# Transposes by the DMA crossbar, joined half chunks and loads cast by DMA in a retention and MLP kernel

## The chip, the cores and the metric

The kernel runs on one core of a Trainium2 chip. A core has five engines with their own instruction streams: TensorE (PE, with weight loads shown apart as PEld), VectorE (DVE), ScalarE (ACT), GpSimd (POOL) and SyncE (SP). Each takes its instructions in order and waits at semaphores. DMAs are issued from SP's and POOL's streams in this kernel and run on sixteen DMA engines that all queues share. The metric is the device time of one execution in microseconds. The time before is 395.73 us, the median of three runs (395.54 to 396.46).

## The reference

There are 8 batches, 8 heads, 576 positions and a head size of 64. First comes retention: scores of q and k, masked to the lower triangle and weighted by a decay per head, times v. The heads side by side give x with 512 columns. Then a mixer of rank 32 over the positions adds to x, which gives u, and an MLP of width 2048 with a ReLU adds to u.

```python
scores = scale * np.matmul(q, k.transpose(0, 1, 3, 2))
gamma = 1.0 - 2.0 ** (-5.0 - np.arange(H, dtype=np.float32))
rel = pos[:, None] - pos[None, :]
Dmat = np.where(rel >= 0, gamma[:, None, None] ** rel[None, :, :], 0.0)
x = np.matmul(scores * Dmat, v)          # heads side by side: (8, 576, 512)
xt = x.transpose(0, 2, 1)
h = xt @ U @ V                           # over the positions, rank 32
u = x + h.transpose(0, 2, 1)
out = u + np.maximum(u @ w_ch1, 0.0) @ w_ch2
```

All inputs and the output are float32; the matrix products run in bfloat16.

## The kernel before

**Decay and state.** The decay is split into a factor of the row and one of the column. v is multiplied on load by `vscale` (the column's factor and the scale), and the result of a chunk by `qscale` (the row's factor). What is left inside a chunk is a triangle of ones, and what comes from earlier chunks is q times a running state, the sum of k transposed times v over those chunks. So a batch is walked in chunks of 128 positions. 576 is four and a half times 128: an even batch ends with a half chunk in partitions 0 to 63, an odd batch begins with one in partitions 64 to 127 (`is_half`, `rows_of`), and two batches of a pair lie in the output as nine full row blocks.

**The front of a batch**, in `attention_items` and `mixer_items`, is a list of small steps for PE, each with its followers on other engines:

- `T(c)`, line 202: eight PE transposes turn a chunk's q and k, head pair by head pair, into one PSUM tile `pst`; ACT copies it to SBUF as `qkT` (line 216).
- `ST(c)`, line 219: four matmuls add k transposed times v to the state in PSUM (`pss`); DVE copies it through a mask `bdm` that keeps the blocks of one head each, as `s_sb` (line 232).
- `SC(c)`, line 238: eight matmuls with 64 contraction rows give the scores, `psc`; DVE multiplies by the triangle, as `ret` (line 257).
- `RV(c)`, line 264: eight matmuls ret x v and four matmuls q x state (128 rows, since the masked state has zeros) gather in `po`; DVE scales to `xt` (line 287).
- `MA(c)`, `MH(c)`, `MT(c)`, lines 319 to 356: the mixer's product with U into `psa`, one copy `a_sb` by ACT, the product with V into `ph`, an addition on DVE that gives `ut`, then four PE transposes into `pu` and an ACT copy into `uT` (line 354).

**The MLP of a batch**, in `mlp_items`: `Y1` takes four matmuls per block of 128 hidden columns from `uT`, with an ACT ReLU; `Y2` takes sixteen matmuls per 128 rows, then DVE adds `ut` and SP stores the 256 KB result. An even batch has four row blocks, an odd one five.

**The order of the work.** PE's order is the program's order (`manual_schedule`): `interleave` mixes the MLP of batch b with the front of batch b + 1 in proportion to estimated costs. The orders on the other engines and on SP are chosen by the framework's scheduler when the program is built. `T` runs two steps ahead of `RV` of the same chunk. Tiles come from pools with fixed numbers of buffers; where a buffer is still in use, the writer waits.

**Loads.** `load_chunk`, line 171: SP loads k, q and v of a chunk as float32 into a staging tile (four buffers), in pieces of 256 bytes; DVE casts q and k to bfloat16 (line 184), POOL scales v (line 185). The weights are loaded by POOL's queue, which casts them while copying (lines 149 and 156). Batches 0 and 1 and the weights are loaded first; the loads of batch b + 2 are placed ahead of the MLP of batch b, and the scheduler runs them as buffers come free (nine of `qkv`).

Of the kernel before, what the change touches and what calls it, by code (L numbers as in the profile page):

```python
# [12 lines left out]
ALU = mybir.AluOpType  # L13
PE = mybir.EngineType.PE


def interleave(main, fill):
# [5 lines left out]
    while i < len(main) or j < len(fill):  # L23
        if j >= len(fill) or (i < len(main) and dm / tm <= df / tf):
            dm += main[i][0]
            main[i][1]()
            i += 1
        else:
            df += fill[j][0]
            fill[j][1]()  # L30
            j += 1
# [3 lines left out]
def kernel(  # L35
# [22 lines left out]
    NC = 5  # L58
    assert S == 4 * P + HALF and B % 2 == 0

# [7 lines left out]
    qkT_pool = ctx.enter_context(tc.tile_pool(name="qkT_pool", bufs=3))  # L68
# [4 lines left out]
    half_pool = ctx.enter_context(tc.tile_pool(name="half_pool", bufs=2))  # L73
# [5 lines left out]
    ps_t = ctx.enter_context(tc.tile_pool(name="ps_t", bufs=1, space=bass.MemoryType.PSUM))  # L79
    ps_sc = ctx.enter_context(tc.tile_pool(name="ps_sc", bufs=1, space=bass.MemoryType.PSUM))  # L80
    ps_s = ctx.enter_context(tc.tile_pool(name="ps_s", bufs=1, space=bass.MemoryType.PSUM))
    ps_o = ctx.enter_context(tc.tile_pool(name="ps_o", bufs=1, space=bass.MemoryType.PSUM))
# [5 lines left out]
    bdm = consts.tile([P, P], BF16, name="bdm")  # L88
    pos = consts.tile([P, NC, H], FP32, name="pos")
    lngt = consts.tile([P, NC, H], FP32, name="lngt")  # L90
    qscale = consts.tile([P, NC, H], FP32, name="qscale")
    vscale = consts.tile([P, NC, H], FP32, name="vscale")
    lnb = consts.tile([P, 1], FP32, name="lnb")
    U_A = consts.tile([P, NC, P], BF16, name="U_A")
    U_B = consts.tile([P, NC, P], BF16, name="U_B")
    Vbig = consts.tile([P, HALF + S + HALF], BF16, name="Vbig")
# [3 lines left out]
    qkvh = [consts.tile([P, 3, H, D], BF16, name=f"qkvh{p}") for p in range(2)]  # L100
    qkTh = [consts.tile([P, 2 * NHP, P], BF16, name=f"qkTh{p}") for p in range(2)]
    reth = [consts.tile([P, H, P], BF16, name=f"reth{p}") for p in range(2)]

    def early_consts():
        make_identity(nc, ident)
        make_upper_triangular(nc, tri, val=1.0, diag=True)
        nc.gpsimd.memset(lnb, math.log(scale))
        nc.gpsimd.iota(
            pos, pattern=[[P, NC], [0, H]], base=0, channel_multiplier=1,
# [4 lines left out]
        nc.vector.tensor_tensor(out=lngt, in0=lngt, in1=pos, op=ALU.mult)  # L114
        nc.scalar.activation(out=qscale, in_=lngt, func=AF.Exp, bias=0.0, scale=1.0)
        nc.scalar.activation(out=vscale, in_=lngt, func=AF.Exp, bias=lnb, scale=-1.0)
        nc.vector.memset(bdm, 0.0)
        for s in range(2):
            nc.vector.memset(bdm[s * HALF:(s + 1) * HALF, s * HALF:(s + 1) * HALF], 1.0)

    def zero_halves():
        for p in range(2):
            nc.vector.memset(qkTh[p], 0.0)
            nc.vector.memset(reth[p], 0.0)
            z = slice(HALF, P) if p == 0 else slice(0, HALF)
            nc.vector.memset(qkvh[p][z, :, :, :], 0.0)

    def late_consts():
        nc.vector.memset(U_A, 0.0)
        nc.vector.memset(U_B, 0.0)  # L130
        nc.vector.memset(Vbig, 0.0)
# [4 lines left out]
        nc.gpsimd.dma_start(out=U_A[0:HALF, 4, 0:R], in_=moe_U[4 * P:S, :])  # L136
        nc.gpsimd.dma_start(out=U_B[HALF:P, 0, 0:R], in_=moe_U[0:HALF, :])
# [54 lines left out]
    def attention_items(b, qkv, x_tiles, pair):  # L192
# [4 lines left out]
        def half_cols(c):  # L197
            if not is_half(b, c):
                return slice(0, P)
# [288 lines left out]
```

## Time and profile before

| What | Value |
|---|---|
| median of three runs | 395.73 us (395.54 to 396.46) |
| the profiled execution | 396.42 us, of which the span of its instructions is 394.6 us |
| busy: PE, weight loads, DVE, ACT, POOL | 348.4, 200.0, 183.1, 156.2, 64.2 us |
| first MLP matmul | 52.84 us |
| first ReLU of the MLPs of batches 0 to 7 | 54.7, 95.4, 142.4, 182.7, 229.6, 269.9, 316.9, 356.3 us |
| PE transposes of q and k | 320 matmuls, evicted by 40 ACT copies of 1.02 us |
| PE transposes of u | 144 matmuls, evicted by 36 ACT copies of 0.60 us |
| DMA queue of SP | 117696 packets, 37.8 MB |
| DMA queue of POOL | 5744 packets, 4.3 MB written |
| read from HBM, written to it | 36.92 MB, 9.44 MB |

The busy table gives each engine's busy time; a busy PE is not PE at its peak, since matmuls are pipelined and their ends are modelled. The forty slices show where in the span an engine is busy. The groups of instructions give one line of the program, its operands and shapes, how often it runs, its busy time with the mean duration of one in nanoseconds, and the idle time ahead of it with what ended that. The DMA issues give the median time from issue to landing. The chain of waits is followed back from the last instruction.

### The profile page before, as it was taken

To read this page: it belongs to the slowest core of one execution; us is meant where nothing else is said; L and a number is where in the kernel's file an instruction comes from. 1 tells how busy PE (TensorE), PEld (TensorE's weight loads), DVE (VectorE), ACT (ScalarE), POOL (GpSimd) and SP (SyncE) were. 2 spreads that over 40 slices of the span, in tenths; PEclk is the share of its full clock that TensorE was granted. 3 is DMA by queue.
4 is the path that set the end of the run, shared out by engine and by line. 5 is a ranking of instruction groups with operands and counts; after the bars stand their busy time and mean duration, and the time that the engine had idled before them with its cause. 6 is when DMAs were issued, how large, how long until landed. Compare 5 with 4: busy or idle time off the path is not lost. (4 is left out here: it accounts for less than half of the span.)

```text
span 394.6 us, 6659 instructions
## 1 busy us (share of the span) xinstructions
PE 348.4 (88%) x2784; PEld 200.0 (51%) x2784; DVE 183.1 (46%) x249; ACT 156.2 (40%) x279; POOL 64.2 (16%) x83
## 2 busy tenths in 40 slices
PE   1244489999999999899999999899999999999996
PEld 0233245446774455446764455346764455456642
DVE  4436326655456555753557445743334533540021
ACT  2121147305770156216760266117750276027700
POOL 6486123301321212210122002200000000000000
PEclk9999959999999999999999999999999999999999
DMA  8999999726995599485149500011001100010012
GB/s 157 217 184 197 198 224 212 131 69 166 223 209 124 150 207 213 98 196 139 25 97 207 140 28 1 28 42 40 2 2 55 55 27 2 28 53 27 2 53 81
DMA packets 123471, 42.49 MB, mean 108 GB/s; under 512 B 114705, under 2 KB 118833, under 8 KB 123441
## 3 DMA queue, kind: packets, MB, share of 16 engines
q1 hardware_dynamic: 117696, 37.76, 43.4%
q0 software_dynamic: 5744, 4.31, 7.2%
q8 instruction: 22, 0.36, 0.4%
q14 instruction: 9, 0.07, 0.1%
HBM read 36.92 MB, written 9.44 MB: 117 GB/s over the span
## 5 line engine op out<-in xcount | busy, mean ns | idle before, releaser
L390 PEld LDWEIGHTS <-w_sb 128*128 128x128 bf16 x768 | 70.4, 98 | 39.1 <-issue 4.7
L185 POOL TENSOR_TENSOR qkv<-stage_t,vscale 128x512 bf16<-128x512 f32 x32 | 34.7, 1085 | 128.3 <-DMA stage_t<-in_v_dram 65.3
L257 DVE TENSOR_TENSOR ret<-psc,tri 128x1024 bf16<-128x1024 f32 x32 | 39.1, 1221 | 9.3 <-PE psc L246 9.1
L328 ACT ACTIVATE a_sb<-psa 128x512 bf16<-128x512 f32 x8 | 4.8, 597 | 97.2 <-PE psa L322 97.2
L184 DVE CAST qkv<-stage_t 128x1024 bf16<-128x1024 f32 x32 | 30.9, 966 | 24.2 <-PE po L270 12.1
L232 DVE TENSOR_TENSOR s_sb<-pss,bdm 128x512 bf16<-128x512 f32 x32 | 22.1, 689 | 41.5 <-PE pss L225 41.5
L216 ACT ACTIVATE qkT<-pst 128x1024 bf16<-128x1024 bf16 x32 | 32.8, 1024 | 20.1 <-PE pst L207 19.1
L287 DVE TENSOR_TENSOR xt<-po,qscale 128x512 bf16<-128x512 f32 x32 | 22.0, 688 | 33.3 <-PE po L277 25.0
L207 PE MATMUL pst<-ident,qkv 128*128 128x128 bf16 x256 | 21.3, 231 | 15.4 <-DVE qkv L184 14.7
L207 PEld LDWEIGHTS <-qkv 128*128 128x128 bf16 x256 | 18.1, 104 | 22.1 <-DVE qkv L184 15.5
L344 DVE TENSOR_TENSOR ut<-ph,xt 128x512 bf16<-128x512 f32 x32 | 22.0, 690 | 11.9 <-PE ph L335 11.7
L270 PE MATMUL po<-qkv,ret 128*128 128x64 bf16 x256 | 13.7, 200 | 8.2 <-DVE ret L257 8.2
L270 PEld LDWEIGHTS <-ret 128*128 128x128 bf16 x256 | 11.6, 102 | 16.9 <-DVE ret L257 13.8
L225 PE MATMUL pss<-qkv 128*128 128x128 bf16 x112 | 11.6, 231 | 6.7 <-POOL qkv L185 6.7
L351 PE MATMUL pu<-ident,ut 128*128 128x128 bf16 x128 | 13.0, 227 | 4.3 <-DVE ut L344 3.8
L351 PEld LDWEIGHTS <-ut 128*128 128x128 bf16 x128 | 10.0, 101 | 12.7 <-DVE ut L344 5.2
L335 PE MATMUL ph<-a_sb,Vbig 128*128 128x512 bf16 x40 | 14.8, 392 | 0.7 <-ACT a_sb L328 0.7
L225 PEld LDWEIGHTS <-qkv 128*128 128x128 bf16 x112 | 9.2, 103 | 11.1 <-issue 6.8
L246 PE MATMUL psc<-qkT 64*128 64x128 bf16 x256 | 13.6, 229 | 0.0
L246 PEld LDWEIGHTS <-qkT 64*128 64x128 bf16 x256 | 7.7, 98 | 11.2 <-issue 11.2
L401 PEld LDWEIGHTS <-y_4127 128*128 128x128 bf16 x80 | 7.8, 98 | 9.3
L277 PE MATMUL po<-s_sb,qkT 128*128 128x128 bf16 x112 | 11.5, 229 | 0.0
(541 smaller groups left out, 615.7 us busy)
## 6 DMA issues: line engine op xcount, KB each, us to landing
out_dram<-o_sb SPq DMA_DIRECT2D x36, 256.0 KB, 2.1
stage_t<-in_k_dram SPq DMA_DIRECT2D x32, 256.0 KB, 4.8
stage_t<-in_q_dram SPq DMA_DIRECT2D x32, 256.0 KB, 4.9
stage_t<-in_v_dram SPq DMA_DIRECT2D x32, 256.0 KB, 5.0
w_sb<-in_moe_w_ch_dram POOLq DMA_DIRECT2D x16, 128.0 KB, 6.7
w_sb<-in_moe_w_ch_dram POOLq DMA_DIRECT2D x8, 256.0 KB, 10.0
stage_t<-in_k_dram SPq DMA_DIRECT2D x8, 128.0 KB, 3.8
stage_t<-in_q_dram SPq DMA_DIRECT2D x8, 128.0 KB, 3.8
```

What stands on the lines that cost most here:

```text
L184: nc.vector.tensor_copy(out=t[rows, 0:2, :, :], in_=f[rows, 0:2, :, :])
L185: nc.gpsimd.tensor_tensor(out=t[rows, 2, :, :], in0=f[rows, 2, :, :], in1=vscale[rows, c, :, None].to_broadcast([L, H, D]), op=ALU.mult,)
L207: nc.tensor.transpose(pst[:, j * NHP + hp, :], t[:, j, 2 * hp:2 * hp + 2, :].rearrange("p h d -> p (h d)"), ident,)
L216: nc.scalar.activation(out=qkT, in_=pst, func=AF.Copy)
L232: nc.vector.tensor_tensor(out=s_sb, in0=pss, in1=bdm[:, None, :].to_broadcast([P, NHP, P]), op=ALU.mult,)
L246: nc.tensor.matmul(psc[:, hl, hp, 0:n], qkT[pb:pb + HALF, NHP + hp, :], qkT[pb:pb + HALF, hp, cols], start=True, stop=True,)
L257: nc.vector.tensor_tensor(out=rv[:, :, :, cols], in0=psc[:, :, :, 0:n], in1=tri[:, None, None, cols].to_broadcast([P, 2, NHP, n]), op=ALU. ...
L270: nc.tensor.matmul(po[:, h * D:(h + 1) * D], ret[:, h, :], t[:, 2, h, :], start=(h == 0), stop=True, skip_group_check=True,)
L287: nc.vector.tensor_tensor(out=xt[rows, :].rearrange("p (h d) -> p h d", d=D), in0=po[rows, :].rearrange("p (h d) -> p h d", d=D), in1=qsca ...
L344: nc.vector.tensor_tensor(out=ut[rows, :], in0=ph[rows, :], in1=x_tiles[c][rows, :], op=ALU.add)
L351: nc.tensor.transpose(pu[:, cc, :], u_tiles[c][:, cc * P:(cc + 1) * P], ident)
L390: nc.tensor.matmul(ps[:, 0:n], w1_sb[:, cc, f * P:(f + 1) * P], uT[:, cc, t0:t0 + n], start=(cc == 0), stop=(cc == NCC - 1),)
```

## The change

Five things are changed together.

1. Nine chunks of 128 rows are walked per pair of batches. The fifth (`XC` = 4) holds the last 64 rows of the even batch and the first 64 of the odd one. Its scores are masked by `trix`, which also cuts across the two halves. The state starts anew at this chunk, from `vx`, a copy of v with the first half zeroed, and q x state uses `qTx`, a copy of q transposed with the second half zeroed; both copies are made by POOL. Group A of a pair is chunks 0 to 4, group B chunks 5 to 8, and the MLPs stay at four and five row blocks.
2. From the second group on, q and k, and u, are transposed by DMAs that SP issues, SBUF to SBUF, in place of PE and ACT. The first group keeps PE transposes, in `ps_big`.
3. q x state is computed next to the scores, in `SC`, as eight matmuls with 64 contraction rows that read only a head's own block of the state. So the mask `bdm` goes, and ACT copies the state in place of DVE. The two heads of a pair go to different PSUM banks of `po`.
4. From the third group on, the loads are issued by POOL and cast while they are copied, straight into `qkv`; POOL then scales v in place. The first two groups are still staged.
5. POOL's order is now the program's order too. The weights come in another order (the first four w1 blocks after the fourth chunk, the others after the first front). `RV` lags one step instead of two, in the first front none; the front mixed into the first MLP begins after 35% of it.

```diff
-def interleave(main, fill):
+def interleave(main, fill, lead=0.0, end=1.0):
...
-        if j >= len(fill) or (i < len(main) and dm / tm <= df / tf):
+        if j >= len(fill) or (
+            i < len(main) and dm / tm <= lead + (end - lead) * df / tf
+        ):
...
-    qkT_pool = ctx.enter_context(tc.tile_pool(name="qkT_pool", bufs=3))
+    qkT_pool = ctx.enter_context(tc.tile_pool(name="qkT_pool", bufs=6))
...
+    def scale_v(t, f, p, c):
+        nc.gpsimd.tensor_tensor(
+            out=t[:, 2, :, :], in0=f[:, 2, :, :],
+            in1=vscale[:, c, :, None].to_broadcast([P, H, D]), op=ALU.mult,
+        )
+        if c == XC:
+            nc.gpsimd.tensor_copy(out=vx[p % 2][HALF:P, :, :], in_=t[HALF:P, 2, :, :])
+
+    def load_chunk(p, c, cast_dma):
+        t = qkv_pool.tile([P, 3, H, D], BF16, tag="qkv", name="qkv")
+        if cast_dma:
+            for j, dram in ((1, k), (0, q), (2, v)):
+                for rows, b, t0 in parts(p, c):
+                    L = rows.stop - rows.start
+                    nc.gpsimd.dma_start(
+                        out=t[rows, j, :, :],
+                        in_=dram[b, :, t0:t0 + L, :].rearrange("h s d -> s h d"),
+                    )
+            scale_v(t, t, p, c)
+            return t
...
         def T(c):
             t = qkv[c]
-            pst = ps_t.tile([P, 2 * NHP, P], BF16, tag="ps_t", name="pst")
-            for j in range(2):
+            qkT = qkT_pool.tile([P, 2 * NHP, P], BF16, tag="qkT", name="qkT")
+            st["qkT", c] = qkT
+            if not pe_transpose:
+                nc.sync.dma_start_transpose(
+                    out=qkT, in_=t[:, 0:2, :, :].rearrange("p j h d -> p (j h d)")
+                )
+                return
...
         def ST(c):
...
-            nc.vector.tensor_tensor(
-                out=s_sb, in0=pss, in1=bdm[:, None, :].to_broadcast([P, NHP, P]),
-                op=ALU.mult,
-            )
+            nc.scalar.activation(out=s_sb, in_=pss, func=AF.Copy)
...
         def SC(c):
...
+            po = ps_o.tile([P, 2, 512], FP32, tag="ps_o", name="po")
+            st["po", c] = po
+            if c > 0:
+                s_sb = st["s", c - 1]
+                qT = qkT
+                if c == XC:
+                    qT = qTx[p % 2]
+                    nc.gpsimd.tensor_copy(
+                        out=qT[:, :, 0:HALF], in_=qkT[:, 0:NHP, 0:HALF]
+                    )
+                for hp in range(NHP):
+                    for hl in range(2):
+                        pb = hl * HALF
+                        nc.tensor.matmul(
+                            po[:, hl, hp * D:(hp + 1) * D],
+                            qT[pb:pb + HALF, hp, :],
+                            s_sb[pb:pb + HALF, hp, pb:pb + HALF],
+                            start=(hp == 0), stop=True, skip_group_check=True,
+                        )
...
         def MT(c):
-            pu = ps_t.tile([P, NCC, P], BF16, tag="ps_t", name="pu")
+            dst = st["uT", par][:, :, (c - c0) * P:(c - c0 + 1) * P]
+            if not pe_transpose:
+                nc.sync.dma_start_transpose(out=dst, in_=st["u", c])
+                return
...
+    with tc.manual_schedule(engines={PE, POOL}):
+        early_consts()
+        for c in A_CH:
+            sts[0]["qkv"][c] = load_chunk(0, c, False)
+            if c == 1:
+                load_mixer()
+            if c == 3:
+                load_w1([0])
+        interleave([], front_items(0, 0, True, 0))
+        load_w1(range(1, dff // W1B))
+        load_w2()
+        load_group(0, 1, False)
+        groups = [(p, par) for p in range(NP) for par in range(2)]
+        for g, (p, par) in enumerate(groups):
+            if g + 2 < len(groups):
+                load_group(*groups[g + 2])
+            fill = front_items(*groups[g + 1]) if g + 1 < len(groups) else []
+            interleave(mlp_items(p, par, sts[p]), fill, 0.35 if g == 0 else 0.0)
```

## The prediction

> **What bounds the kernel now.** I read the busy table and the 40 slices first. TensorE (PE) is 88% busy; only the first slices leave it idle, and there the DMA row is full.
>
> ```profile
> PE 348.4 (88%) x2784; PEld 200.0 (51%) x2784; DVE 183.1 (46%) x249; ACT 156.2 (40%) x279; POOL 64.2 (16%) x83
> ...
> PE   1244489999999999899999999899999999999996
> ...
> DMA  8999999726995599485149500011001100010012
> ```
>
> Next the timeline about the first MLP matmul: the MLP begins at 52.84 us, and its matmuls of 512 columns start 0.43 us apart, twice as far as later; the clock records stand at a half until 57.7 us.
>
> ```profile
> 52.84 1.87 PE L390 MATMUL ps_y_553<-uT_474,w_sb 128*128 128x512 bf16 x4 [0.69 <-ACT uT_474 L354]
> ```
>
> Stages (columns: window, length, busy time of PE, weight loads, DVE, ACT, POOL, granted clock, DMA share, GB/s): the half clock in the second, and one stage later on where PE stands 1.9 us.
>
> ```profile
> 40.00:50.00 10.00, 5.36 (x29) 2.52 (x30) 3.35 (x6) 1.54 (x3) 2.08 (x2) 0.87 1.08 203
> 50.00:60.00 10.00, 8.80 (x50) 4.85 (x48) 3.35 (x6) 5.14 (x8) 2.58 (x3) 0.62 1.09 221
> ...
> 160.00:170.00 10.00, 8.11 (x79) 3.99 (x78) 8.02 (x8) 1.02 (x2) 2.90 (x3) 1.00 0.37 91
> ```
>
> From then on the chain of waits is PE work end to end; its steps (start, length) give prices: a transposed chunk of q and k (T) 0.45 us, four u transposes 0.22, state matmuls 0.22, scores 0.33 (and 0.11 more in the next piece), ret x v 0.23, four MLP matmuls 0.86.
>
> ```profile
> 263.29 0.22 PE pu L351 x4
> 263.51 0.86 PE ps_y_3011 L401 x4
> ...
> 272.52 0.54 PE ps_y_3184 L390 x4
> 273.06 0.45 PE pst L207 x8
> ...
> 275.14 0.22 PE pss L225 x4
> 275.36 0.54 PE ps_y_3225 L390 x4
> 275.90 0.33 PE psc L246 x8
> 276.23 0.65 PE ps_y_3242 L390 x4
> ...
> 279.50 0.23 PE po L270 x8
> ```
>
> Last, the groups and DMA issues that the change rebuilds. POOL waits 65 us for landings of v, at no cost today, because SP runs the loads ahead into four staging tiles.
>
> ```profile
> L185 POOL TENSOR_TENSOR qkv<-stage_t,vscale 128x512 bf16<-128x512 f32 x32 | 34.7, 1085 | 128.3 <-DMA stage_t<-in_v_dram 65.3
> ...
> stage_t<-in_v_dram SPq DMA_DIRECT2D x32, 256.0 KB, 5.0
> w_sb<-in_moe_w_ch_dram POOLq DMA_DIRECT2D x16, 128.0 KB, 6.7
> ```
>
> **PE work removed.** After the first group (now "g0" to "g7", two per pair of batches, whose MLPs start at M0 to M7) the fronts lose 35 x T = 15.8 us, 32 u transposes x 0.22 = 7.0, and, by four half chunks joined into 31 chunks in place of 35, 1.0 of scores and 0.9 of ret x v: 24.7 us. The row tiles of q x state are priced by the half chunks' scores, eight 64-column row tiles in 0.22 us, which is what four full matmuls take now: nothing won. Two tiles at a time would save 0.1 each, the 0.11 that scores leave in the piece after them would be lost again: 31 x 0.1 = 3 us to either side. An even group's MLP with the next front is then 34.5 us: four chunks x 32 matmuls of 512 columns x 0.216 = 27.65, and for the front 4 x (0.44 + 0.23 + 0.22 + 0.22) + 11 mixer matmuls x 0.216 = 6.8. An odd one's is 41.7: 34.6 + 5 x (0.44 + 0.23) + 8 x 0.22 + 9 x 0.216.
>
> **Start.** Group 0 loads without weights beside it. 1024 packets of 256 B take 1.2 us when the SP queue is alone (1700 per 2 us), so a chunk takes 3.6 us, and the fifth lands at about 23 (U, V and the first four w1 blocks come between). From the last q, about 22 us, the chain is cast 0.7, T 1.0, eviction 1.0, POOL copy 0.6, ret 1.2, ret x v 0.6, xt 0.7, psa and a_sb 1.2, four MH/MT rounds of 1.5: M0 = 35.5, against 52.8.
>
> **Boundaries.** Today the last u transpose goes PE, ACT (0.60), PE: 0.65 us idle. Afterwards it is ut 0.69, an SP issue and a landing. No row has a crossbar transfer; the nearest is the output store, 256 KB on the same queue, 2.0 us. Bounds: below, 2.0 (a u tile has half the bytes); above, the staged loads of many pieces, 5.0. I take 2.5, nearest to the store. About one Y2 block (0.86) covers some of it: 0.8 + 2.5 - 0.86 = 2.5 us, 1.9 more than today. DVE loses the casts that held ret in the 160-170 row (1.9 us idle), and I give 1.0 per group for that. ACT gives up 36 + 19 us of evictions and takes 19 of state copies; it binds nothing. Group periods: 34.5 + 2 (today's stalls) + 1.9 - 1 = 37.5 and 44.7. If nothing else bound, the span would be 35.5 + cold clock and late loads 5 + four times 37.5 + three times 44.7 + the last MLP with its tail 39.2 (as today) - 1 = about 363 us.
>
> **The new chain: loads on POOL.** From group 2 on 27 chunks, 90 DMAs, leave SP and its staging, and POOL issues k, q and v itself, then waits for v in order, scales it, and only then reaches the next chunk's DMAs. Behind that wait stand all later loads and the qTx copy. One link r: first packet 2.06 us after the issue (first w1 block: 1.82 to 3.88), 3072 packets, 0.57 to landing (V block), scaling 1.09 and some 0.1. A packet took 26.4 ns where 128 B were cast to 64 (U blocks) and 20.7 ns for 256 B uncast, on each of 16 engines; a cast of 256 B lies between, so I take 23.5: 4.5 us, and r = 8.3. Bounds: 18 ns (the median of the uncast) gives 7.3; 26.4 ns with 2 us of transposes in between gives 10.9.
>
> It starts late. POOL first scales group 1's last chunk. Weights and staged loads alternate packet by packet (320 each per 2 us in 28 to 44 us), so group 1 gets a fifth of its rate beside them. Of 4096 weight packets 512 go from 22 to 26 and the others, issued after the qTx copy, from 27.5 at 160 per us: they end at 50. By then about 400 + 1700 + 3600 of group 1's 12288 packets have moved; 6600 remain, 7.8 us. It lands at 58, and T0 = 59.5.
>
> **What waits for it.** The built instruction order of SP puts the five qkT transposes of group 2 before group 1's u transposes, and those of chunks 0 and 1 of group 4 before the output stores of group 1's MLP and the u transposes of group 2. SP waits in order, so M1 cannot come before chunk 4 of group 2: T0 + 4r + 12 (q landed 6, the transposes and a store ahead 3.5, landing 2.5) = 104.7, against 78 from PE (35.5 + 34.5 + 5 + 2.5); then 2 for a half clock after idle time, as the 4.8 us at half rate cost above. M2 cannot come before chunk 1 of group 4: T0 + 1 + 10r + 14.7 = 158.2 (the last term is q 5.8, transpose 1, then a store to free the third output tile 2.5, an output add and three u adds 2.8, transpose 2.6); by PE it would be 106.7 + 44.7 = 151.4. Later bounds are met (M3: 190 against 195.7). After M2: 37.5 + 44.7 + 37.5 + 44.7 + 37.5 + 39.2 = 241.1. Sum: 399.3 us of span, against 394.6. The profiled execution took 1.8 us beyond its span and stood 0.7 above the median of 395.73; with both, **400.4 us**, 1.2% slower.
>
> **Where the skill weighs in.** The Trainium skill, "DMA: Bandwidth & Descriptors", section "Anatomy of one DMA — SWDGE (gpsimd) path", fits a POOL DMA as 2.0 us plus bytes over 436 GB/s. An estimate from it: 786 KB of a chunk in 3.8 us with the fixed part, r about 5.0 with scaling, the M2 bound gone, and a span near 380, a gain. Against the change speaks the same page's "Specifications": pieces under 512 B miss line rate, and the cast writes 128 B pieces. The packet rows agree with the second (256 B in 20.7 ns on 16 engines are 198 GB/s), and they decide.
>
> **Rivals.**
> (a) *The chain is shorter, and the kernel faster.* With r = 7.3 M2 falls to 148.2, and the PE path from M1 = 100.7 gives the same: 148.2 + 241.1 = 389.3, 390.4 with the rest. It turns at r = 7.8. For it: 18 ns medians; against it, the cast rows.
> (b) *The loads keep ahead and PE bounds it:* 363 + 1 = 364. It needs the chain to start by 35 us or r under 4; three landings in a row with 2.06 us ahead speak against it.
> (c) *The crossbar is slow.* If a q/k transpose holds the queue like a staged load of as many bytes and lands in 5 us, each boundary costs 2.5 more, and its packets lengthen r to 10: M2 = 175, + 241 + 5 x 2.5 = 429, 430.
> (d) The change does what it says: the transposes leave PE in the built order; only their worth is open.
>
> **How the numbers follow.** Forecast (r 7.95 to 9.7, 396.9 to 415): 0.50. (a): 0.22. (b): 0.13. (c) and r over 9.7: 0.12. Within 0.3%, about what a measurement of this kernel can tell from no change: 0.03. Faster is (a) + (b) = 0.35; slower 0.62. The likeliest's own range is 397 to 415. The range leaves 0.2 out: below 383 lies (b), 0.13; above, r = 10.4 with two more us of landing gives 423, and 0.07 of (c) lies beyond.
>
> **What would show it.** Right: PE idle some 25 us before M1, ended by DMA uT, and SP before it waiting for qkT of group 2; POOL waits for qkv<-in_v_dram in its own tile, 4 us or more each; MLP starts near 36, 105, 158; PE busy about 325 us. Wrong: POOL links under 7 us, PE at 9 in all slices from 40 us on, or boundary waits over 4 us.

## The result and the profile after

The changed kernel takes 411.07 us (median; 406.13 to 412.71) against 395.63 us before: a ratio of 1.035, 95% interval 1.0251 to 1.0448. It is slower. The forecast was 400.4 us, between 383 and 423. Medians here are of all executions of a kernel; ratios and intervals leave out the slow ones, more than 1.5% above its fastest.

The profiled execution took 411.97 us, its span is 410.2 us. First the busy line of PE and three rows of the 40 slices: PE's work is there in less busy time (329.0 us against 348.4), but its row has a deep hole in slices 9 to 11 and dips at the boundaries after it, the granted clock falls with them, and the DMA row stays full until slice 28, but for slice 24. The second fence is the clock row of the kernel before, which dips once.

```profile
PE 329.0 (80%) x2406; PEld 179.1 (44%) x2440; DVE 126.0 (31%) x172; ACT 123.5 (30%) x244; POOL 137.4 (33%) x176
...
PE   2554948950499987997899969993999979988995
...
PEclk9999987985599996999899989996899989999999
DMA  9999999999999999999999949999120220031011
```

```profile
PEclk9999959999999999999999999999999999999999
```

The waits of PE (us in total, times, longest) say who holds it. One wait of 21.0 us stands ahead of M1. The smaller waits for uT are the boundaries ahead of M2 to M6 (M5 has two), and the wait for qkT is the first crossbar transpose of group 1.

```profile
PE ps_y_940 L429 <- DMA uT<-ut: 21.0, 1, 21.0
...
PE psc L265 <- DMA qkT<-qkv: 6.1, 1, 6.1
...
PE ps_y_2783 L429 <- DMA uT<-ut: 4.0, 1, 4.0
...
PE ps_y_1469 L429 <- DMA uT<-ut: 3.5, 1, 3.5
PE ps_y_2383 L429 <- DMA uT<-ut: 3.4, 1, 3.4
PE ps_y_1854 L429 <- DMA uT<-ut: 3.3, 1, 3.3
...
PE ps_y_2768 L429 <- DMA uT<-ut: 3.0, 1, 3.0
PE ps_y_3268 L429 <- DMA uT<-ut: 2.8, 1, 2.8
```

The timeline of SP's queue ahead of M1 (start, length, what) shows the order that the prediction spoke of: the qkT transpose of group 2's chunk 4 goes first, at 97.01, as soon as POOL's load of it has landed, and only then the five u transposes of group 1, whose u had been ready since 88.4. The same order returns ahead of M2: a qkT transpose of group 4 at 143.76, three output stores that had stood behind it, then u. M1 begins at 108.31, M2 at 155.83.

```profile
97.01 1.23 SPq L225 DMA_TRANSPOSE qkT<-qkv  x1
98.34 0.52 SPq L447 DMA_DIRECT2D out_dram<-o_sb  x1
98.95 5.34 SPq L393 DMA_TRANSPOSE uT<-ut  x4
...
143.76 1.23 SPq L225 DMA_TRANSPOSE qkT<-qkv  x1
145.09 1.50 SPq L447 DMA_DIRECT2D out_dram<-o_sb  x3
148.20 1.23 SPq L393 DMA_TRANSPOSE uT<-ut  x1
```

POOL's waits, the scaling of v (busy, mean ns) and the DMA issues (KB each, median us to landing) give the chain's link: POOL waits 27 times for v and scales in 1.04 us. Where little else was on its way, the next chunk begins some 7.2 us after the last; beside other transfers a link took up to 9.7 us, and the mean over all 27 chunks is 8.3.

```profile
POOL qkv L183 <- DMA qkv<-in_v_dram: 111.1, 27, 6.0
...
L183 POOL TENSOR_TENSOR qkv<-qkv,vscale 128x512 bf16<-128x512 bf16 x27 | 28.0, 1037 | 111.1 <-DMA qkv<-in_v_dram 111.1
...
qkv<-in_k_dram POOLq DMA_DIRECT2D x24, 128.0 KB, 3.6
qkv<-in_q_dram POOLq DMA_DIRECT2D x24, 128.0 KB, 4.6
qkv<-in_v_dram POOLq DMA_DIRECT2D x24, 128.0 KB, 4.6
...
uT<-ut SPq DMA_TRANSPOSE x32, 2.9
qkT<-qkv SPq DMA_TRANSPOSE x31, 3.1
```

### The profile page after: what moved, and what is told of

It is laid out like the page before. It is cut to its first block, busy times and chain, and to the rows that moved or that the text cites. A ratio compares the mean times of both kernels' runs of the same rounds, so it can differ in the third digit from the quotient of the medians.

```text
span 410.2 us, 5915 instructions
## 1 busy us (share of the span) xinstructions
PE 329.0 (80%) x2406; PEld 179.1 (44%) x2440; DVE 126.0 (31%) x172; ACT 123.5 (30%) x244; POOL 137.4 (33%) x176
## 4 chain that ended last, share of the span: by engine, by line
PE 67%; DMA 11%; issue 8%; POOL 7%; SPq 3%; DVE 2%; ACT 1%; POOLq 0%; DVEq 0%
DMA uT<-ut 6%; POOL qkv L197 3%; PE psc L265 3%; POOL qkv L183 2%; DMA w_sb<-in_moe_w_ch_dram 2%; PE po L305 2%; SPq L393 2%; PE psa L364 2%; PE pss L248 1%; POOL w_sb L169 1%; PE ph L382 1%; DMA stage_t<-in_v_dram 1%; DMA U_A<-in_moe_U_dram 1%; SPq L207 1%; PE ps_y_3231 L440 1%
## 5 line engine op out<-in xcount | busy, mean ns | idle before, releaser
L429 PEld LDWEIGHTS <-w_sb 128*128 128x128 bf16 x768 | 74.4, 103 | 96.0 <-issue 38.0
L183 POOL TENSOR_TENSOR qkv<-qkv,vscale 128x512 bf16<-128x512 bf16 x27 | 28.0, 1037 | 111.1 <-DMA qkv<-in_v_dram 111.1
L197 POOL DMA_DIRECT2D qkv<-in_k_dram x30 | 26.9, 899 | 7.9 <-PE pss L248 7.9
L197 POOL DMA_DIRECT2D qkv<-in_v_dram x30 | 25.9, 869 | 0.0
L197 POOL DMA_DIRECT2D qkv<-in_q_dram x30 | 25.6, 857 | 0.0
L255 ACT ACTIVATE s_sb<-pss 128x512 bf16<-128x512 f32 x32 | 19.0, 593 | 4.1 <-PE pss L248 3.9
L305 PEld LDWEIGHTS <-ret 128*128 128x128 bf16 x288 | 13.7, 102 | 12.5 <-DVE ret L292 6.8
L183 POOL TENSOR_TENSOR qkv<-stage_t,vscale 128x512 bf16<-128x512 f32 x9 | 9.3, 1046 | 21.8 <-DMA stage_t<-in_v_dram 17.6
L248 PEld LDWEIGHTS <-qkv 128*128 128x128 bf16 x128 | 11.9, 115 | 8.1 <-issue 3.0
L211 DVE CAST qkv<-stage_t 128x1024 bf16<-128x1024 f32 x9 | 6.3, 702 | 22.1 <-DMA stage_t<-in_q_dram 22.1
L440 PEld LDWEIGHTS <-y_3632 128*128 128x128 bf16 x80 | 7.8, 98 | 9.3
L440 PEld LDWEIGHTS <-y_2767 128*128 128x128 bf16 x80 | 7.6, 98 | 8.6
L440 PEld LDWEIGHTS <-y_939 128*128 128x128 bf16 x80 | 7.6, 98 | 8.6
```

The source lines that it names most:

```text
L183: nc.gpsimd.tensor_tensor(out=t[:, 2, :, :], in0=f[:, 2, :, :], in1=vscale[:, c, :, None].to_broadcast([P, H, D]), op=ALU.mult,)
L197: nc.gpsimd.dma_start(out=t[rows, j, :, :], in_=dram[b, :, t0:t0 + L, :].rearrange("h s d -> s h d"),)
L248: nc.tensor.matmul(pss[:, hp, :], t[:, 1, 2 * hp:2 * hp + 2, :].rearrange("p h d -> p (h d)"), vt[:, 2 * hp:2 * hp + 2, :].rearrange("p h ...
L255: nc.scalar.activation(out=s_sb, in_=pss, func=AF.Copy)
L305: nc.tensor.matmul(po[:, hl, hp * D:(hp + 1) * D], ret[:, h, :], t[:, 2, h, :], start=(c == 0 and hp == 0), stop=True, skip_group_check=True,)
L429: nc.tensor.matmul(ps[:, 0:n], w1_sb[:, cc, f * P:(f + 1) * P], uT[:, cc, t0:t0 + n], start=(cc == 0), stop=(cc == NCC - 1),)
```

## The experiments

Two theories were put to the chip. **A**: M1 and M2 are late because of what stands ahead of what in queues that work in order, fed by POOL's chain of loads. **B**: the rest is paid at the boundaries, where PE waits for a crossbar transfer that nothing covers and then runs at half the clock. Against A stood that the loads themselves are too late, however the queues stand. The starts of the MLPs, read from the timeline of each kernel's trace (first matmul that reads uT, us), carry most verdicts:

| kernel | M0 | M1 | M2 | M3 | M4 | M5 | M6 | M7 | span |
|---|---|---|---|---|---|---|---|---|---|
| before | 52.8 | 94.7 | 141.3 | 181.9 | 228.6 | 269.2 | 315.9 | 355.6 | 394.6 |
| after | 42.2 | 108.3 | 155.8 | 196.0 | 242.2 | 281.0 | 332.2 | 369.2 | 410.2 |
| e1_end | 42.3 | 104.1 | 156.5 | 193.8 | 237.3 | 276.2 | 320.2 | 355.4 | 394.3 |
| e2_sp | 42.1 | 92.4 | 156.1 | 197.1 | 245.0 | 286.6 | 335.6 | 374.2 | 417.5 |
| e3_staged | 42.2 | 110.5 | 164.8 | 201.8 | 248.1 | 284.7 | 332.4 | 369.3 | 412.2 |
| e4_upe | 42.0 | 88.7 | 151.5 | 188.2 | 231.1 | 267.8 | 310.7 | 347.5 | 386.7 |
| e5_warm | 42.4 | 109.2 | 157.2 | 196.6 | 243.0 | 283.2 | 329.6 | 367.4 | 406.4 |
| e8_qtx | 42.2 | 102.0 | 151.3 | 189.8 | 232.7 | 273.4 | 316.3 | 353.1 | 392.4 |
| e9_g1 | 42.1 | 104.0 | 148.0 | 190.3 | 233.1 | 275.6 | 318.5 | 355.4 | 394.1 |
| e10_act | 42.5 | 107.6 | 158.3 | 199.9 | 252.2 | 294.4 | 344.7 | 380.1 | 423.1 |
| e11_dve | 52.4 | 92.6 | 152.0 | 188.8 | 231.7 | 268.5 | 311.4 | 348.2 | 387.5 |
| e12_order | 52.1 | 92.9 | 140.7 | 178.5 | 225.9 | 270.5 | 319.4 | 358.9 | 397.8 |
| e13_best | 42.1 | 83.3 | 132.6 | 169.3 | 212.2 | 249.0 | 291.8 | 328.6 | 367.3 |
| e14_cross | 42.4 | 85.6 | 130.7 | 166.2 | 207.7 | 243.9 | 288.9 | 326.8 | 366.3 |

**The front ends before the MLP (e1_end).**

```diff
-            interleave(mlp_items(p, par, sts[p]), fill, 0.35 if g == 0 else 0.0)
+            interleave(mlp_items(p, par, sts[p]), fill, 0.35 if g == 0 else 0.0, 0.82)
```

> Edit: in every group the front of the next group is spread over the first 82% of the MLP instead of all of it, so that its last u transposes are issued some 7 us before the MLP ends. No work is added or left out. Theory A (the 21 us hole ahead of M1 is SP's queue: u transposes stand behind the five qkT transposes of group 2, which wait for POOL's chain of loads): the hole stays, M1 near 108, because the queue is the same. Theory B (the rest of the loss is the crossbar's wait at each boundary, 2.8 to 7 us, and the half clock that follows it): the waits ahead of M2 to M7 shrink from about 21 us together to under 5, the granted clock stays at 1.0 there (some 10 us more), so 411 becomes 383 to 392. Rival to B (the fronts themselves are slower: waits for landed q and k, for state copies or for a PSUM tile): the waits only move from the boundary into the MLP, 405 to 413.

Measured: 395.44 us, 0.9975 of before (0.9942 to 1.0007), some 16 us less than the changed kernel and level with the kernel before. M1 comes at 104.1, 4 us sooner, and M2 at 156.5; from M2 to the end it takes 237.8 us instead of 254.4. That is B's share: a boundary costs little once the u transposes land under the rest of the MLP. Waits of 5.4, 1.9 and 3.6 us remain (M2, M3, M5), so the time lies above the 383 to 392 us that B gave. The hole ahead of M1 only shrinks, its wait from 21.0 to 15.0 us, and M2 does not come sooner: as A says, the holes stay.

**SP in the order of the text (e2_sp).**

```diff
-    with tc.manual_schedule(engines={PE, POOL}):
+    with tc.manual_schedule(engines={PE, POOL, SP}):
```

> Edit: SP's instructions are issued in the order of the program text, like PE's and POOL's, so that the u transposes of a group stand in SP's queue ahead of the qkT transposes of the group after it. No work is added or left out. Theory A (the hole ahead of M1 is the order of SP's queue): M1 comes 3 to 4 us after the MLP of g0 ends, near 91 instead of 108, the later boundary waits of about 3.3 us and the half clock after them stay, total 391 to 396. Rival A2 (POOL's loads themselves are too late for PE, whatever SP's order): the hole moves into the front of group 2, M2 stays at 153 to 157, total 407 to 413.

Measured: 423.95 us, 1.0587 (1.0547 to 1.0628): slower still. M1 comes at 92.4, so its hole was the order in SP's queue. But M2 does not move. PE now waits inside the MLP for the copy qTx of the middle chunk's q, which POOL makes only after it has issued, awaited and scaled all four chunks of group 3; the timelines of POOL and PE:

```profile
130.41 1.04 POOL L184 TENSOR_TENSOR qkv<-qkv,vscale 128x512 bf16<-128x512 bf16 x1 [3.75 <-DMA qkv<-in_v_dram]
131.40 0.39 POOL L279 COPY qTx<-qkT 128x256 bf16<-128x256 bf16 x1
...
131.84 0.40 PE L285 MATMUL po<-s_sb,qTx 64*128 64x64 bf16 x8 [7.91 <-POOL qTx L279]
```

And the boundaries grow from about 3.3 to between 4 and 6 us, for in this order an output store that waits for its o_sb can stand ahead of a u transpose, and qkT transposes follow at once behind. Neither theory had foreseen a slower kernel.

**All loads staged again (e3_staged).**

```diff
-    def load_group(p, par, cast_dma=True):
+    def load_group(p, par, cast_dma=False):
```

> Edit: all loads go back to staging tiles (loaded uncast by SP, cast by DVE, v scaled and cast by POOL), as group 1's are; transposes by the crossbar, joined chunks and row tiles stay. Adds 27 DVE casts (about 0.7 us each, off PE's path). Theory A as stated (POOL's chain of load, wait, scale holds qkT of group 2): without that chain group 2 is loaded sooner, M1 comes at 91 to 98, total 393 to 402; boundary waits stay. Rival A2 (any queue that carries loads and transposes together holds the transposes as long): now SP holds both, the staged loads wait for free tiles ahead of the transposes in the same queue, M1 at 108 or later and boundary waits over 4 us, total 411 to 425.

Measured: 413.68 us, 1.0426 (1.038 to 1.0472): the rival's case by its time, but of its boundary waits only those at M1 and M2 (4.1 and 6.5 us) pass the 4 us that the rival gave; the others are 1.3 to 2.9. The hole is only moved, from M1 into group 1's front, where the first qkT transpose now stands in SP's queue behind fifteen more staged loads:

```profile
80.40 0.61 PE L265 MATMUL psc<-qkT 64*128 64x128 bf16 x8 [23.77 <-DMA qkT<-qkv]
```

So the cast loads on POOL are not the fault by themselves. With the loads on SP, the transposes stand behind loads; with the loads on POOL, the u transposes stand in SP behind qkT transposes that wait for loads.

**u by PE (e4_upe).**

```diff
-            if not pe_transpose:
+            if False:
                 nc.sync.dma_start_transpose(out=dst, in_=st["u", c])
```

> Edit: only the u transposes go back to PE with an ACT eviction in all groups (32 times 0.22 us of PE, 7 us); q and k stay on the crossbar, loads stay cast on POOL. If both theories hold (A: the u transposes wait in SP's queue ahead of M1; B: their landing and the half clock cost each boundary 4 to 5 us), M1 comes at 88 to 90, boundary waits fall to 0.7 us, the clock stays at 1.0, total 411 - 20 - 18 - 11 + 7 = 369, range 365 to 380. If the loads themselves are late (A2): M2 stays at 153 to 157 and only the boundaries are won, 385 to 395. If neither: 411 to 418, with the PE work added.

Measured: 390.11 us, 0.9834 (0.9796 to 0.9872). M1 comes at 88.7 and no boundary waits over 0.8 us; from M2 to the end it is 235 us, 19 less than the changed kernel although PE has 7 us more to do. M2 stays at 151.5: PE waits once more for qTx, 17.85 us, behind POOL's loads.

```profile
127.83 1.04 POOL L183 TENSOR_TENSOR qkv<-qkv,vscale 128x512 bf16<-128x512 bf16 x1 [3.40 <-DMA qkv<-in_v_dram]
128.82 0.39 POOL L278 COPY qTx<-qkT 128x256 bf16<-128x256 bf16 x1
...
129.26 0.39 PE L284 MATMUL po<-s_sb,qTx 64*128 64x64 bf16 x8 [17.85 <-POOL qTx L278]
```

The time also lies in the branch that was kept for loads that are too late, and M2 of 151 to 157 in four kernels with different M1 looks like it. To decide, e8_qtx and e9_g1 below take that copy off POOL.

**The clock held up (e5_warm).** PE runs matmuls that nothing reads while it waits at a boundary.

```diff
+            if 0 < g < len(groups) - 1:
+                warm = ps_big.tile([P, 512], FP32, tag="ps_big", name="warm")
+                for i in range(16):
+                    nc.tensor.matmul(warm, w1_sb[:, i % NCC, 0:P], w2_sb[:, i, :], ...)
```

> Edit: at the six boundaries ahead of M2 to M7 PE runs 16 matmuls of 512 columns into a PSUM tile that nothing reads, in the time in which it waits for the last u transposes; the rest as in the changed kernel. Adds 96 matmuls, 21 us at the full clock, of which about 3.3 us per boundary lie in the wait. Theory B (the half clock after each boundary is what the 3 us of standing costs on top): the clock stays at 1.0 after the boundaries, 1.4 to 2.7 us less each, less some 0.3 us by which the added matmuls end late: total 400 to 406 instead of 411. Rival (the clock falls for another reason, or the pace after a boundary is set by loads and evictions): 411 to 414.

Measured: 408.07 us, 1.0277 (1.0241 to 1.0313), 3 us below the changed kernel. That is a smaller gain than expected, and the two intervals overlap, so the reading rests on the trace. Windows over the starts of M2 to M4, first of the changed kernel and then of this one (window, length, busy time of PE, weight loads, DVE, ACT, POOL, granted clock, DMA share, GB/s):

```profile
152.00:162.00 10.00, 6.54 (x38) 2.86 (x36) 0.93 (x2) 2.47 (x5) 5.07 (x6) 0.66 1.07 139
192.00:202.00 10.00, 6.69 (x46) 4.14 (x44) 2.45 (x3) 3.23 (x8) 3.69 (x4) 0.83 1.49 168
238.00:248.00 10.00, 6.47 (x42) 3.13 (x42) 1.94 (x3) 2.77 (x5) 4.14 (x6) 0.83 0.66 96
```

```profile
152.00:162.00 10.00, 8.72 (x60) 4.03 (x59) 2.10 (x3) 2.81 (x5) 3.69 (x4) 1.00 1.31 154
192.00:202.00 10.00, 8.48 (x69) 5.14 (x67) 1.56 (x2) 3.67 (x9) 3.69 (x4) 1.00 1.28 132
238.00:248.00 10.00, 8.39 (x59) 3.95 (x57) 1.86 (x2) 2.90 (x6) 4.47 (x7) 1.00 1.30 118
```

The clock column goes from 0.66 and 0.83 to 1.00, and the MLPs of g2 to g6, first matmul to last output add, shrink by 2.4, 1.4, 1.4, 1.2 (beyond the 4.0 us of the second wait, which is gone) and 1.3 us: 7.6 us in all. That is the price of the half clock, 1.2 to 2.4 us for each pause of 2.8 to 3.5 us, and a little too low: at M5, after a wait of 2.29 us, the clock stood at a half for 3.4 us in this kernel too. The gain is smaller, since the pauses from the last Y2 to M2, M3, M4 and M5 became 4.8 to 5.9 us long (16 added matmuls and then a further wait of 1.2 to 2.3 us). Ahead of M4, for one, the u transposes landed 4.3 to 6.4 us after issue, where the changed kernel's took 2.4 to 2.9. That they met more of the cast loads is likely from the timing, but was not tested.

**qTx copied by DVE (e8_qtx), and group 1's q and k by PE as well (e9_g1).** Both stand on e4_upe.

```diff
-                    nc.gpsimd.tensor_copy(
+                    nc.vector.tensor_copy(
                         out=qT[:, :, 0:HALF], in_=qkT[:, 0:NHP, 0:HALF]
```

and e9_g1 besides

```diff
-            p, A_CH if par == 0 else B_CH, st, pe_t, lag
+            p, A_CH if par == 0 else B_CH, st, pe_t or (p, par) == (0, 1), lag
```

> Edit: u transposed by PE, as in the kernel e4_upe, and the copy of the middle chunk's q (qTx) made by DVE instead of POOL. Theory A3 (two chains bind M1 and M2 one behind the other: the u transposes in SP's queue, taken away in e4_upe, and then the qTx copy, which stands in POOL's program order behind group 3's loads; PE waited 17.8 us for it): the 17.8 us go, nothing takes their place, total 390 - 17.8 = 372, range 367 to 376. Rival A4 (the loads themselves are too late, and the next wait for q, k or v takes its place): the hole moves to the next qkT transpose or state matmul, total 382 to 390.

> Edit: as e8_qtx, and q and k of group 1 alone transposed by PE (four chunks, 4 x 0.45 = 1.8 us of PE), because SP's queue held that group's first crossbar transpose 12 us behind staged loads (PE waited 4.7 to 6.1 us, and the clock stood at a half after it). Expected: that wait goes, 4.7 + 1 to 3 of half clock - 1.8, so 3 to 6 us below e8_qtx. Rival (group 1's q and k land too late for either way): the same time as e8_qtx or up to 2 us more.

Measured: 394.52 us, 0.9945 (0.9925 to 0.9965), and 397.3 us, 0.9986 (0.9953 to 1.0019): both miss. PE's wait for qTx is gone, but the built order had put the copy into DVE's queue ahead of u adds of the group before, and DVE waited there for the qkT transpose of group 2's chunk 4:

```profile
98.17 0.24 DVE L278 COPY qTx<-qkT 128x256 bf16<-128x256 bf16 x1 [13.76 <-DMA qkT<-qkv]
98.33 0.68 DVE L388 TENSOR_TENSOR ut<-ph,xt 128x512 bf16<-128x512 f32 x1
```

M1 slid back to 102. In e9_g1 the wait for group 1's first qkT did vanish (PE came to the same point 6.6 us sooner), and the hole ahead of M1 grew from 12.3 to 18.3 us: PE reached the same gate earlier.

**u on the crossbar from ACT's queue (e10_act).**

```diff
-                nc.sync.dma_start_transpose(out=dst, in_=st["u", c])
+                nc.scalar.dma_start_transpose(out=dst, in_=st["u", c])
```

> Edit: the u transposes stay on the crossbar but are issued by ACT's queue instead of SP's, and the qTx copy is made by DVE. No PE work is added. If the crossbar's landing and issue at each boundary are the whole price of u on the crossbar (theory B) and A3 holds, M1 comes at 91 to 92 and M2 at 135, boundaries of about 3.3 us and the half clock after them stay: 372 - 7 + 7 x 3 + 7 x 1.8 = 399 at most, 385 to 399. If issuing from ACT holds up its evictions (each issue took SP 1.2 us), boundary waits grow over 5 us: 400 to 412. If the waits shrink below 2 us, because ACT issues a transpose sooner after the add: 375 to 385.

Measured: 427.18 us (421.81 to 433.17; no interval was formed), the worst of all and above all three forecasts. M1 again at 107.6, after a wait of 23.3 us. DVE's early qTx copy is one reason (its wait is 15.1 us here). The issues show another: transposes of the two queues never overlap. SP's transpose of chunk 4 landed at 98.40 and ACT's first followed at 98.47; ACT's last landed at 108.33 and SP's next followed at 108.44. The turns are in the program as built: SP's transposes wait at a semaphore that the landing of uT raises, which cost SP 31.2 us in 12 waits:

```profile
SPq L225 <- DMA uT<-ut: 31.2, 12, 7.1
```

So a second queue was no way out as the kernel was built. What two queues in flight at once would do is not shown, and the two reasons were not tried apart. The Trainium skill, "DMA: Bandwidth & Descriptors", section "DMA Transpose (X-bar)", says that two streams of transposes in flight together can spoil each other's data and have to be serialized by waiting for completion; the waits agree with that rule, and no run here shows the harm.

**DVE in the order of the text (e11_dve).** As e8_qtx, with

```diff
-    with tc.manual_schedule(engines={PE, POOL}):
+    with tc.manual_schedule(engines={PE, POOL, DVE}):
```

> Edit: as e8_qtx (u by PE, qTx copied by DVE), with DVE's instructions issued in the order of the program text. In e8_qtx the built order had put the qTx copy ahead of the u adds of the group before, so the 17.8 us ahead of the qTx matmuls came back as 12.3 us ahead of M1 and 4.3 ahead of M2. Theory A3 (the holes at M1 and M2 are a matter of what stands in an in-order queue ahead of what, and the loads are early enough): both holes go, M1 88 to 90, M2 near 130 to 132, total 390 - 17.8 = 372, range 367 to 377. Rival A4 (loads too late): a new wait of 8 us or more for qkT or qkv, 380 to 390.

Measured: 389.91 us, 0.986 (0.9818 to 0.9902): a miss that named the third gate. After M1 at 92.6 (M0 is 10 us later, because in this order all five casts of group 0 stand ahead of its first ret on DVE), PE stood 15 us ahead of M2, for u. DVE stood for 16.84 us at an output add, which needs one of three o_sb tiles back; SP issued that tile's store only at 143.13, because the qkT transpose of group 4's chunk 1 was ahead of it in its queue:

```profile
145.56 0.69 DVE L447 TENSOR_TENSOR o_sb<-ps_y,ut 128x512 f32<-128x512 f32 x1 [16.84 <-DMA out_dram<-o_sb]
146.17 0.68 DVE L389 TENSOR_TENSOR ut<-ph,xt 128x512 bf16<-128x512 f32 x1
```

```profile
141.79 1.23 SPq L226 DMA_TRANSPOSE qkT<-qkv  x1
143.13 3.48 SPq L448 DMA_DIRECT2D out_dram<-o_sb  x4
```

This is the path that the prediction gave for M2. The time is one that the rival had named, but the cause is not: the chain of loads feeds three gates, SP's queue for u at M1, POOL's for qTx and SP's for the output stores at M2, and the last two give nearly the same M2, 148 to 156. Each kernel so far removed one or two of the three.

**Orders alone, u on the crossbar (e12_order).** SP and DVE in the order of the text, qTx by DVE, the front within 82% of the MLP.

```diff
-    with tc.manual_schedule(engines={PE, POOL}):
+    with tc.manual_schedule(engines={PE, POOL, SP, DVE}):
```

> Edit: everything that the change moved to the crossbar stays there, u too; only orders are changed: SP's and DVE's instructions in the order of the program text, the qTx copy by DVE, and the front spread over the first 82% of each MLP. If order alone is what the change lacked (theory A3 for the holes, theory B for the boundaries), M1 comes at 88 to 92, boundary waits stay under 2 us and the clock at 1.0: e11_dve less the 7 us of u transposes on PE, plus some 1 us per boundary, 365 to 378. If the crossbar cannot deliver beside the loads (transposes of 4 to 7 us, one issue per 1.2 us): boundary waits of 2 to 5 us remain, 380 to 400.

Measured: four executions between 386.03 and 401.42 us, too far apart for a verdict. The profiled one took 399.6 us. In its trace M2 comes at 140.7, no gate of 15 us is left at M1 or M2, and PE waits six times, 21.3 us in all, for the first qkT of a group: a transpose written right before its use is issued too late:

```profile
PE psc L267 <- DMA qkT<-qkv: 21.3, 6, 6.1
```

The boundaries wait 1.5 us at most, as the lower forecast wanted, but this other wait, which neither forecast had, keeps the time above it. It also has e11_dve's late M0.

**All three gates taken away (e13_best).** On e4_upe: SP in the order of the text with each qkT transpose written two chunks ahead (the first two of a group already at the end of the front before), the qTx copy on POOL behind the first chunk of the following loads instead of behind all four, group 1's q and k by PE.

```diff
-    with tc.manual_schedule(engines={PE, POOL}):
+    with tc.manual_schedule(engines={PE, POOL, SP}):
...
-                add(T, chunks[s], 460 if pe_transpose else 0)
+                if pe_transpose:
+                    add(T, chunks[s], 460)
+                else:
+                    for ahead in chunks[s:s + 3]:
+                        add(T, ahead, 0)          # T(c) does nothing a second time
...
                 add(SC, c, 520)
+                if c == XC and rest:
+                    items.append((0, rest))       # the other three chunks of group g + 2
...
+        if early:
+            items.append((0, early))              # T of the first two chunks of group g + 2
```

> Edit: as e4_upe (u by PE; q, k on the crossbar; loads cast on POOL), with the three in-order queues put in a better order. SP: its instructions in the order of the text, each qkT transpose written two chunks ahead of its use, the first two of a group ahead of the MLP before it. POOL: the qTx copy stands behind the first chunk of the group loaded after it instead of behind all four. Group 1's q and k by PE (1.8 us). No data is left out. Theory A5 (M1 and M2 were held by queue order in turn: u behind qkT, qTx behind loads, and output stores behind the qkT of group 4, so that DVE could not write o_sb): no hole over 3 us from M0 on. From the undisturbed periods of e4_upe (36.4 and 43.2 us, last MLP with its tail 39.6): M0 43, M1 84, M2 127, end 127 + 235 = 362, 364 with what lies around the span, range 361 to 372. Rival A4 (POOL's loads, one chunk per 7.3 us from 62 us on, are too late for PE however the queues stand): M2 at 140 to 152 again, 376 to 390.

Measured: 368.92 us, 0.9253 (0.9219 to 0.9288). The holes are gone: M1 83.3, M2 132.6, and PE is at nine from slice 6 on, but for slice 12 and the tail. One wait over 1 us remains after M0, 3.8 us for qTx, which stands behind one chunk's load; with the half clock after it M2 comes 5.6 us later than expected.

```profile
PE 333.4 (91%) x2600; PEld 182.1 (50%) x2600; DVE 126.4 (34%) x172; ACT 145.7 (40%) x280; POOL 137.4 (37%) x176
...
PE   2565799999959999999999999999999999999995
```

The chain of loads is as it was, in the mean one chunk per 8.3 us as in the changed kernel. The rival to A, loads too late for PE, is out. What each edit is worth alone was not measured.

**The same with u on the crossbar (e14_cross).**

```diff
-            if False:
+            if not pe_transpose:
                 nc.sync.dma_start_transpose(out=dst, in_=st["u", c])
...
-            interleave(mlp_items(p, par, sts[p]), fill, 0.35 if g == 0 else 0.0)
+            interleave(mlp_items(p, par, sts[p]), fill, 0.35 if g == 0 else 0.0, 0.82)
```

> Edit: as e13_best, with u on the crossbar in all groups after the first, from SP's queue, and the front spread over the first 82% of each MLP so that the u transposes land under its end. 7 us less PE work than e13_best. Theory B2 (with the queue in order and the boundary covered, the crossbar is worth its PE work): no boundary wait over 1.5 us, clock at 1.0, 2 to 7 us below e13_best. Rival (the transposes beside loads, 4 to 7 us each and one per 1.2 us in SP, still end behind the MLP, or delay the qkT transposes behind them): waits of 2 to 6 us at some boundaries or at the first scores of a group, 5 to 20 us above e13_best.

Measured: 363.71 us, 0.9162 (0.9125 to 0.9199), the fastest; its interval lies under that of e13_best. In the one that was profiled (368.03 us, so above the median) PE waits three times for uT:

```profile
PE ps_y L440 <- DMA uT<-ut: 3.8, 3, 2.3
...
PE ps_y L440 <- issue: 3.2, 1, 3.2
```

One of the three is 2.3 us, ahead of M1, and 3.2 us ahead of M6 have no releaser in the profile; M6's last u transpose landed at 288.80, and M6 began at 288.89. The clock stood at a half for 3.4 us after M1 and for 6.8 after M6. So in this execution B2's conditions, waits of at most 1.5 us and a clock of 1.0, were not met, though the time that it named, 2 to 7 us below e13_best, was. With the queues in order and the boundary mostly covered the crossbar is worth its PE work: by the ratios (0.9253 - 0.9162) x 396.1 = 3.6 us of the 7 removed (the earlier end of the front is part of this kernel, and was not tried alone on e13_best). All that the change moved to the crossbar is on it, but for group 1's q and k.

## Why the prediction was right, and where its sizes were off

The cause was right, and rival (d) came true: the transposes leave PE, and what is lost is order, not work. The holes lie where the forecast put them. That the direction came out clear of noise is partly luck. The chain of loads ran faster than priced: with its measured times (T0 62.05; group 4's chunk 1 issued at 138.37) the forecast's own terms behind it, 14.7 + 241.1 + 1.1, give 395.3 us, no change. The slowdown came from terms that were priced too low. The span missed by 10.9 us: M2 came 2.4 sooner than forecast, and 13.3 were lost behind it. Term by term, the forecast first:

- **PE work.** An even group 34.5 us, an odd one 41.7. Measured where the clock holds (e5_warm, first matmul of an MLP to the start of its last output add): 34.5, three times, and 41.5. The term held. That the row tiles win nothing did not quite: the two matmuls of a pair start 3 ns apart, and the scores with q x state take 0.45 us (302.09 to 302.53) where the scores alone took 0.33 and q x state's four full matmuls 0.22 in the kernel before, some 0.1 us for each.
- **Start, M0.** 35.5 (the terms listed add to 35.0); measured 42.2. The last q landed at 21.2 (22 in the forecast), but chunk 4's transposes began only at 27.3, since DVE and PE were still busy with chunk 3; the chain was priced as if the last chunk met idle engines. Its four rounds of u cost 1.82 us each, not 1.5. It is 6.7 us of error that M1 swallowed, because M1 hung on the loads.
- **T0 and r.** 59.5 and 8.3; measured 62.05, and some 7.2 where little else moved. The ten links to M2's gate took 7.6 us each. In the link from 77.38 the first packet moved 1.65 us after issue (2.06 in the forecast), its 3072 packets moved in 4.2 us (4.5), the landing took 0.3 (0.57) and the scaling 1.0. A packet took 33.2 ns in the mean, not 23.5; end to end on 16 engines 3072 of them would take 6.4 us, so packets overlapped. Rival (a), which is an r of 7.3, came nearly true, but its 389 us did not, since it needed the other terms to hold. The Trainium skill's fit ("DMA: Bandwidth & Descriptors", section "Anatomy of one DMA — SWDGE (gpsimd) path") had led to an r of about 5; for the 256 KB that one cast load reads it gives an estimate of 2.6 us (2.0 + 0.6), and these landed in 3.6 to 4.6 (medians).
- **M1.** 104.7, with 2 of cold clock behind it; measured 108.3. Four links took 29.7 us instead of 33.2, the q load landed 5.2 after them instead of 6, and the qkT transpose of chunk 4 issued at 97.01. From there to M1 it took 11.3 us instead of 6: the five u transposes leave SP one per 1.3 us, and the last four land in 4.7 to 6.6 us beside the loads. The gate was right, its tail was too short.
- **M2.** 158.2; measured 155.8, by the path named (and e11_dve shows it alone). The near hit is partly luck: group 4's chunk 1 was issued 5.1 us sooner than forecast, and from its qkT transpose at 143.76 to M2 it took 12.1 us instead of 8.9. The forecast did not price the third gate: it says that the qTx copy stands behind POOL's loads, but gives it no time. It was worth 17.85 us in e4_upe and hidden in the changed kernel.
- **After M2.** 241.1; measured 254.4. This is the mis-sized term. Five boundaries were priced at 2.5 us with the clock at one. The waits at M3 to M7 were 3.31, 3.37, 3.00 + 4.04, 2.84 and 1.26 + 1.91, 19.7 in all instead of 12.5, and the half clock that follows a pause, priced only at M1, took at least 7.6 us by e5_warm over g2 to g6. The two together, 14.8, are a little more than the 13.3 lost. One of the prediction's signs of being wrong showed here: the second wait at M5 passed 4 us.
- **Not priced.** The first qkT transpose of group 1 held SP for 10.6 us behind staged loads and PE for 6.07.
- **Signs.** PE stood 21.0 us ahead of M1 (some 25 forecast), SP before it waited for qkT of group 2, and PE was busy for 329.0 us (325). POOL's waits for v are under 4 us in 16 of 27 links, though 4 or more was named for each.

The clock, as the rows show it: after the pauses ahead of M3, M4 and M6, 2.8 to 3.4 us long, its records stand at a half for 3.4 us, after those ahead of M2 and M5 for 6.8 and 10.2, while after e4_upe's boundaries of under 0.8 us it stood at 1.0. The Trainium skill, "TensorE: Matmul & The Clock Gate", section "Part 1: The HAM clock gate (the "warmup" mystery)", says that the clock halves after an idle window of some 3.4 us and takes one busy window to come back. The half clock after M3, M4 and M6 has that length; the pause need not. Pauses of 2.84 us here, 2.29 in e5_warm (M5) and 2.33 in e14_cross (M1) were enough, while one of 2.93 in e3_staged (M4) passed without, and the measurements decide.

## What to carry to other kernels

Before work is moved to a DMA queue, write down what stands ahead of it in that queue and what each of those entries waits for; a transpose that is cheap in itself takes on the lateness of everything before it. When a removed wait comes back elsewhere with the same end, look for a second and a third gate on the same feed before concluding that the feed is too slow: the holes here closed only when SP's and POOL's orders were both changed and nothing late stood ahead of DVE's adds. In this case a pause of 3 us on PE cost 4 to 5, for the clock that follows it.

## What was not expected of the hardware

- A crossbar transpose costs the issuing queue 1.2 us, alike for 128x512 (u) and 128x1024 (qkT), so a run of them leaves one per 1.3 us (five u of e14_cross took 6.6 us, 77.20 to 83.84). Landing, undisturbed, was 2.4 us for u and 3.05 for qkT; beside cast loads many took 4 to 7 us.
- Loads cast by DMA from 256 B to 128 B pieces took 33.2 ns a packet in the mean, more than the uncast 256 B pieces of the kernel before (20.7) and more than 64 B written (26.4). Packets overlapped: 3072 of them moved in 4.2 us on 16 engines.
- Transposes written for two queues came out of the build with waits for each other's landing: SP stood 31.2 us at them in e10_act.
